# Staging the FFN weights deeper and decoding them four halves per three units, with one more attention tile on the fp32 path, in a fused bias-attention, layer-norm and FFN kernel

## The chip, the core and the metric

The kernel runs on one core of one Trainium2 chip. The metric is the device time of one launch in microseconds (us). The engines are TensorE (PE in the profile), VectorE (DVE), ScalarE (ACT), GpSimd (POOL) and SyncE (SP); SP and POOL are used here mostly to issue DMAs.

## The reference, cut to what matters

Attention with a position bias over 4 batches (B), 8 heads (H), 576 positions (S) and 64 columns per head (D), then a layer norm and a feed-forward network (FFN) with a residual:

```python
scores = scale * np.matmul(q, k.transpose(0, 1, 3, 2))          # per batch and head, 576 x 576
x = (psi_rel / psi_i)[..., None]                                # from the positions alone
h = np.maximum(x @ w1 + b1, 0.0)                                # hidden 32
scores = scores + (h @ w2).transpose(2, 0, 1)[None]             # one bias per head, all batches
attn = np.exp(scores - np.max(scores, axis=-1, keepdims=True))
attn = attn / (np.sum(attn, axis=-1, keepdims=True) + 1e-09)
x = np.matmul(attn, v).transpose(0, 2, 1, 3).reshape(B, S, 512)
xn = (x - mu) / np.sqrt(var + 1e-06) * g_ln
out = x + np.maximum(xn @ w_ch1, 0.0) @ w_ch2                   # w_ch1 512 x 2048 and w_ch2 2048 x 512, float64
```

The two FFN weights come as 64-bit floats. The kernel reads their raw 32-bit words and builds 32-bit floats from them on DVE.

## The kernel before, in words

**Units and tiles.** The attention is cut into 144 units (b, c, h): a batch, a chunk of 128 query rows and a head. Chunk 4 holds the last 64 rows, two heads to a unit, four units to a batch. `ORD` lists the 20 (batch, chunk) pairs in their order; units are numbered through it, 0 to 143. For unit u, `qk` puts the scores into PSUM (`sps`, L390); `softmax1` adds the bias `ldb` and takes the row maximum in one DVE instruction (L414, the landmark for a unit from here on) and takes the exponential on ACT (L418); `softmax2` and `pv` turn the probabilities round and multiply them with v. The finished rows of a (batch, chunk) pair, 18 tiles in all since the chunks 4 of two batches share one, go through `ln1` and `ln2`, and then are one "block" of the FFN.

**Two paths for the probabilities.** Pairs in the set `NAT` keep fp32: `softmax2` turns them on PE with five transposes (L436, L437), ACT copies the result to SBUF (L438, L439), and `pv` multiplies with raw v in fp32 (L486, or L503 for chunk 4). All others go to fp16 in two parts: ACT writes the high part (L423), DVE the low part (L442, L444), SP issues a DMA transpose (L447, `pt<-e`), and `pv` runs 18 fp16 matmuls (L457) against v that `split_v` has split in two (L341 for the maximum, L368 for the low part).

**The weights.** They come in 16 slices f of two halves i (`w_ch1` and `w_ch2`), 32 halves of 512 KB of raw words. `load_w` issues a half on SP. `decode_w` builds the floats with three DVE instructions (L602, L604, L606) into `wslot[f + 1]`, and PE adds the half to a Gram matrix that bounds the weights (L615). Once all eight halves of a group of four slices are decoded, `w_scale` sets the group's scale, and `split_w` writes the fp16 high part on ACT (L641) and the low part on DVE (L644) into `wslot[f]`. Raw words stand in two places only (`wslot[NF - 1]` and `wslot[NF]`, the two ends of tile `wend`), and the load of one half is issued when the half two before it has been decoded. The main loop decodes one half in each unit:

```python
for _ in range(8):
    if wdec and 32 - len(wdec) < 1 + (100 * u) // 100:
        f, i = wdec.pop(0)
        decode_w(f, i)
        ...
        if wload:
            load_w(*wload.pop(0))
```

**The FFN.** A job is one block with one weight group: 48 matmuls of `ffn_w1` into `hps` (L667), the ReLU and its split into `hh` (ACT L672, DVE L675), 12 matmuls of `ffn_w2` into `y` (L695), and the sum into x (`ffn_y`, DVE L706). There are 72 jobs. `next_fs` takes the first job whose block has passed its layer norm and whose group is split. The main loop paces them: it counts up `mbank` so that the jobs of all blocks that are ready are done by the time the next block comes, at most two half jobs per unit.

**Bias.** `bias_relu` (DVE and ACT L172, L174) and `bias_mm` (PE L210) make the bias of 16 query rows for all heads, `nb<-ev` (L220) writes it to memory in the layout of the diagonal, and `ldb<-nb` (L324 to L327) reads it back per head. The first seven groups come ahead of unit 0.

**What sets the order.** The code is unrolled; a scheduler of the framework puts the instructions of each engine in one fixed order, which the engine keeps at run time. Buffers come from pools of fixed depth. `after` adds a wait by hand; `gate` collects loads that have to wait for a bias group of the start.

Of the kernel before, what the change touches and what calls it, by code (L numbers as in the profile page):

```python
# [22 lines left out]
def kernel(  # L23
# [83 lines left out]
    wslot = [wp.tile([128, 1024], F32, name=f"w{f}") for f in range(NF - 1)]  # L107
# [71 lines left out]
    def bias_mm(gi):  # L179
# [17 lines left out]
        else:  # L197
# [21 lines left out]
        dst = dst.rearrange("k (h j) -> k h j", h=NH)[:, :, 0:ntot]  # L219
        SY.dma_start(out=dst, in_=ev[:, 0:ntot])  # L220

    ORD = [(0, 4), (1, 4), (0, 0), (1, 0), (2, 0), (3, 0), (3, 4), (2, 4),
           (2, 1), (3, 1), (1, 1), (0, 1), (0, 2), (1, 2), (3, 2), (2, 2),
           (2, 3), (3, 3), (1, 3), (0, 3)]
    units, ustart, vis = [], {}, []
    for n, (b, c) in enumerate(ORD):
        ustart[b, c] = len(units)
# [7 lines left out]
    gend = {c: sum(len(range(8 * x, min(36, 8 * x + 8))) for x in corder[:corder.index(c) + 1])  # L235
            for c in range(5)}

    NAT = {(0, 4), (1, 4), (0, 0)}

    def nat_pv(b, c):  # L240
        return (b, c) in NAT
# [31 lines left out]
    gate, gate_on = [], [True]  # L273
# [294 lines left out]

        defer(lo)

    wraw = {}

    def load_w(f, i):
        if f < NF - 2:
            dst = wslot[NF - 1 + i]
        elif f == NF - 2 and i == 1:
            dst = wslot[NF]
        else:
            dst = [ep.tile([128, EW], F32, tag="e", name="wst")[:, 0:512] for _ in range(2)]
            for j in range(2):  # L580
                ld = SY.dma_start(
                    out=dst[j].bitcast(U32),
                    in_=w_ch[f].bitcast(U32)[:, 1024 * i + 512 * j:1024 * i + 512 * j + 512])
                after(ld, ttri[max(ttri)])
            wraw[f, i] = dst
            return
        ld = SY.dma_start(out=dst.bitcast(U32), in_=w_ch[f].bitcast(U32)[:, 1024 * i:1024 * i + 1024])
        if gate_on[0]:
            gate.append((ld, 1 + 2 * i))
        if f >= NF - 2:  # L590
            after(ld, ttri[max(ttri)])
        wraw[f, i] = dst

    def decode_w(f, i):
        wf = wslot[f + 1][:, 512 * i:512 * i + 512]
        src = wraw.pop((f, i))
        src = src if isinstance(src, list) else [src]
        nw = 512 // len(src)
        for j, raw in enumerate(src):
            raw = raw.bitcast(U32).rearrange("p (a b) -> p a b", b=2)  # L600
            w = wslot[f + 1][:, 512 * i + nw * j:512 * i + nw * j + nw].bitcast(U32)
            V.tensor_scalar(out=w, in0=raw[:, :, 1], scalar1=3, scalar2=0x3FFFFFFF,  # L602
                            op0=ALU.logical_shift_left, op1=ALU.bitwise_and)
            V.scalar_tensor_tensor(out=w, in0=raw[:, :, 0], scalar=29, in1=w,  # L604
                                   op0=ALU.logical_shift_right, op1=ALU.bitwise_or)
            V.scalar_tensor_tensor(out=w, in0=raw[:, :, 1], scalar=0xC0000000, in1=w,  # L606
                                   op0=ALU.bitwise_and, op1=ALU.bitwise_or)
        g = GOF[f]
        f0, f1 = GROUPS[g]
        if g not in gram:  # L610
            gram[g] = ps_y.tile([128, 512], F32, tag="y1", name="gram")
        wb = wf.bitcast(BF16).rearrange("p (a b) -> p a b", b=2)[:, :, 1]
        for c in range(4):
            blk = wb[:, 128 * c:128 * c + 128]
            T.matmul(out=gram[g][:, 128 * i:128 * i + 128], lhsT=blk, rhs=blk,  # L615
                     start=(f == f0 and i == 0 and c == 0), stop=(f == f1 - 1 and i == 1 and c == 3))
# [152 lines left out]
    gate.append((SY.dma_start(out=gs_sb, in_=g_r), 3))  # L769
    wload = [(f, i) for f in range(NF) for i in range(2)]  # L770
    wdec = list(wload)
    for _ in range(2):
        load_w(*wload.pop(0))
    issue_loads(-6)
    V.memset(mhalf, -0.5)
    V.memset(one_sb, 1.0)
    V.memset(half2, 0.5)
    bias_setup()
    issue_loads(-4)
    NP = 7  # L780
# [41 lines left out]
    u = 0  # L822
    while u < NU + 6 or jobs or cur_job or pend or yq:
        if u >= NEARLY:
            ffn_y()
        softmax1(u)
        issue_loads(u)
        softmax2(u - 1)
        flush()
        for _ in range(8):  # L830
            if wdec and 32 - len(wdec) < 1 + (100 * u) // 100:
                f, i = wdec.pop(0)
                decode_w(f, i)
                if i == 1 and f + 1 == GROUPS[GOF[f]][1]:
                    w_scale(GOF[f])
                if wload:
                    load_w(*wload.pop(0))
        while mm_done[0] < ngroup:
            bias_mm(gorder[mm_done[0]])
            mm_done[0] += 1  # L840
        if u % 2:
            qk(u + 1)
            qk(u + 2)
        while npv <= u - LAG:
            if pv(npv):
                lnq.append([u, len(avail_at) + len(lnq)])
            npv += 1
        for fn in todo.pop(u, []):
            fn()
        for g, (f0, f1) in enumerate(GROUPS):  # L850
            if wdone[0] >= 2 * f1 and g not in wready_at:
                wready_at[g] = u
        if u < NU + 9:
            nav = len([a for a in avail_at if a <= u])
            goal = sum(2 * NF * len(bl) // 4 for bl in blocks if bl[-1] < nav)
            nxt = min((steps_av[bl[-1]] for bl in blocks if bl[-1] >= nav), default=NU + 9)
            mbank += max(0.0, (goal - (ntot - nmicro) - mbank)) / max(1, nxt - u)
            mbank = min(mbank, 2.0)
        else:
            mbank = 1.0  # L860
        flush_lo()
        ffn_y()
        while mbank >= 1.0:
            if not ffn_micro(u):
                break
            mbank -= 1.0
            nmicro -= 1
            if mbank >= 1.0:
                ffn_y()
        bneed = NP + 1 + u if u < 8 else 12  # L870
        for c in (1, 2, 3):
            bneed = max(bneed, gend[c] - 8 + min(8, (u - cfirst[c] + 30) * 8 // 26))
        if ngroup < min(36, bneed):
            bias_relu(gorder[ngroup], 1)
            ngroup += 1
        for _ in range(2):
            if wspl:
                split_w(*wspl.pop(0))
        for it in list(lnq):
            if it[0] == u - 1:  # L880
                ln1(it[1])
# [57 lines left out]
```

## Time and profile before

| | before |
|---|---|
| time, median of 3 runs | 746.67 us (737.48 to 750.48) |
| profiled execution | 743.11 us |
| its span, first to last instruction | 741.3 us |
| PE busy | 651.0 us |
| DVE busy | 489.6 us |
| ACT busy | 380.9 us |
| mean granted TensorE clock, share of full speed | 0.929 |

The profile is of one execution, so sums are made against 743.11 us, of which 1.8 us lie outside the span; the median of the runs is 3.6 us above that execution. Busy time of PE counts matmuls with their modelled ends, so a busy PE need not be one at its peak.

### The profile page before, as it was taken

The numbers are of one execution on the slowest core, as the hardware profiler recorded it, in microseconds if no ns is written. First come the engines' busy times: TensorE is split into PE (matmuls) and PEld (weight loads), VectorE is DVE, ScalarE is ACT, GpSimd is POOL, SyncE is SP. The second block draws the span as 40 slices with busy tenths as digits, with TensorE's granted clock in tenths as the row PEclk, the third lists the DMA queues.
The fourth block names the chain that finished last, engine by engine and source line by source line (L and its number), as shares of the span: only waits on it lengthen the run. The fifth ranks groups of instructions, "written<-read, shape, count | busy, mean of one in ns | idle before, by whom it ended". The sixth has DMA issues, their size and how long they took to land. (4 is left out here: it accounts for less than half of the span.)

```text
span 741.3 us, 19318 instructions
## 1 busy us (share of the span) xinstructions
PE 651.0 (88%) x7980; PEld 445.9 (60%) x7980; DVE 489.6 (66%) x1114; ACT 380.9 (51%) x731; POOL 87.0 (12%) x160
## 2 busy tenths in 40 slices
PE   4368887576669999999988969999998999999997
PEld 3134465444456766766755647667666767676774
DVE  4467789987788657766585746575675666767322
ACT  4255874453257555556475735566765445454110
POOL 3301120100110010101110101011001101000000
PEclk9668997658969999999999989999999999999999
DMA  7987977699627688977768799686859777646100
GB/s 258 362 241 224 342 239 194 144 234 202 148 61 144 119 154 206 220 153 174 172 107 159 141 191 187 144 178 152 165 118 238 194 150 159 110 81 126 31 16 15
DMA packets 200909, 123.30 MB, mean 166 GB/s; under 512 B 175860, under 2 KB 176116, under 8 KB 200820
## 3 DMA queue, kind: packets, MB, share of 16 engines
q1 hardware_dynamic: 190676, 88.32, 57.0%
q0 software_dynamic: 9280, 33.56, 14.9%
q8 instruction: 63, 1.03, 0.6%
q10 hardware_dynamic: 864, 0.18, 0.2%
q14 instruction: 26, 0.21, 0.1%
HBM read 63.92 MB, written 15.64 MB: 107 GB/s over the span
## 5 line engine op out<-in xcount | busy, mean ns | idle before, releaser
L667 PE MATMUL hps<-xT,w 128*128 128x128 f16 x3240 | 207.1, 225 | 6.9 <-DVE hh L675 3.8
L667 PEld LDWEIGHTS <-w 128*128 128x128 f16 x3240 | 192.4, 101 | 20.2 <-issue 10.2
L418 ACT ACTIVATE t<-t,m 128x576 f32<-128x576 f32 x144 | 111.0, 771 | 179.2 <-DVE m L414 177.7
L695 PE MATMUL y<-w,hh 128*128 128x512 f16 x810 | 190.8, 384 | 1.5 <-DVE x L706 0.8
L442 DVE SCALAR_TENSOR_TENSOR e<-t,e 128x512 f16<-128x512 f32 x128 | 88.2, 689 | 71.4 <-ACT e L423 71.0
L695 PEld LDWEIGHTS <-hh 128*128 128x128 f16 x864 | 80.4, 99 | 89.4 <-issue 4.9
L414 DVE CUSTOM_DVE_ANT_0 t<-sps,ldb 128x576 f32<-128x576 f32 x144 | 107.1, 753 | 25.5 <-PE sps L390 17.4
L390 PE MATMUL sps<-kf,qf 64*128 64x288 f32 (+1 forms) x640 | 104.9, 468 | 8.0 <-DVE m L414 7.8
L457 PE MATMUL xps<-v,pt 128*128 128x64 f16 (+1 forms) x1904 | 79.7, 198 | 31.1 <-DMA pt<-e 26.3
L457 PEld LDWEIGHTS <-pt 128*128 128x128 f16 (+1 forms) x1904 | 66.3, 102 | 64.5 <-issue 32.8
L423 ACT ACTIVATE e<-t 128x576 f16<-128x576 f32 x128 | 86.3, 679 | 12.0 <-DMA pt<-e 9.3
L706 DVE SCALAR_TENSOR_TENSOR x<-y,ycs,x 128x512 f32<-128x512 f32 x72 | 53.9, 749 | 48.3 <-PE y L695 48.1
L672 ACT ACTIVATE hh<-hps 128x512 f16<-128x512 f32 x72 | 42.1, 584 | 69.2 <-PE hps L667 69.2
L390 PEld LDWEIGHTS sps<-kf,qf 64*128 64x128 f32 (+1 forms) x640 | 49.2, 187 | 42.3 <-issue 12.6
L675 DVE SCALAR_TENSOR_TENSOR hh<-hps,hh 128x512 f16<-128x512 f32 x72 | 49.4, 687 | 35.5 <-ACT hh L672 35.1
L291 POOL DMA_DIRECT2D kf<-in_k_s_dram x64 | 36.0, 562 | 262.6 <-PE sps L390 237.8
L172 ACT ACTIVATE r<-psi_sb,pr_sb 128x512 f32<-128x512 f32 (+31 forms) x92 | 52.7, 633 | 6.4 <-DVE pr_sb L123 3.7
L210 PE MATMUL bps<-r,nw_sb 128*32 128x296 f32 (+34 forms) x474 | 34.1, 368 | 11.3 <-DVE r L174 9.9
L602 DVE TENSOR_SCALAR w<-wend 128x512 uint32<-128x512 uint32 x28 | 12.1, 431 | 34.7 <-DMA wend<-in_w_ch_dram 34.7
L304 POOL DMA_DIRECT2D qf<-in_q_main_dram x32 | 17.6, 551 | 120.2 <-PE sps L390 80.0
L210 PEld LDWEIGHTS bps<-r,nw_sb 128*32 128x32 f32 x474 | 16.7, 118 | 21.8 <-issue 10.4
L641 ACT ACTIVATE w<-w,ws 128x512 f16<-128x512 f32 x28 | 19.7, 716 | 17.7 <-DVE ws L113 9.8
(102 smaller groups left out, 548.0 us busy)
## 6 DMA issues: line engine op xcount, KB each, us to landing
kf<-in_k_s_dram POOLq DMA_DIRECT2D x64, 288.0 KB, 4.4
wend<-in_w_ch_dram SPq DMA_DIRECT2D x29, 512.0 KB, 5.7
nb<-ev SPq DMA_DIRECT2D x33, 296.0 KB, 3.6
ldb<-nb SPq DMA_DIRECT2D x32, 288.0 KB, 5.3
qf<-in_q_main_dram POOLq DMA_DIRECT2D x32, 256.0 KB, 4.7
vf<-in_v_p_dram POOLq DMA_DIRECT2D x16, 320.0 KB, 8.0
out_dram<-x SPq DMA_DIRECT2D x18, 256.0 KB, 2.8
ldb<-nb SPq DMA_DIRECT2D x16, 144.0 KB, 8.2
```

The lines of the kernel that those rows point to most:

```text
L172: S.activation(r[:, 0:n], psi_sb[:, 0:n], AF.Relu, bias=pr_sb[:, g4:g4 + 1], scale=1.0)
L210: T.matmul(out=ps[32 * s:32 * s + 32, hf, a - lo:b - lo], lhsT=nw2_sb, rhs=src, start=True, stop=True)
L390: T.matmul(out=o, lhsT=l, rhs=kk, start=True, stop=True, tile_position=(64 * hf, 64 * e))
L414: ttri[u] = V.tensor_tensor_reduce(out=halves(t), in0=ps[:, :, 0:HS], in1=halves(bias), scale=-0.125, scalar=3e38, op0=ALU.add, op1=ALU.mi ...
L418: S.activation(t, t, AF.Exp, bias=m, scale=-1.0, accum_out=l8[b, c][:, h:h + 1])
L423: S.activation(e16[:, 0:SEQ], t, AF.Copy, scale=E_SCALE)
L442: V.scalar_tensor_tensor(out=e16[:, 640:1152], in0=t[:, 0:512], scalar=E_SCALE, in1=e16[:, 0:512], op0=ALU.mult, op1=ALU.subtract)
L457: T.matmul(out=o, lhsT=p[:, m], rhs=v[:, j, a, :], start=(i == 0), stop=(i == len(ops) - 1))
L667: T.matmul(out=h[:, idx * n:idx * n + n], lhsT=w[:, wo + kk * 128:wo + kk * 128 + 128], rhs=xT[k][:, xo + kk, 0:n], start=(i == 0), stop=( ...
L675: V.scalar_tensor_tensor(out=hh[:, 1], in0=h, scalar=0.0, in1=hh[:, 0], op0=ALU.max, op1=ALU.subtract)
L695: T.matmul(out=yps[k][t], lhsT=hh[:, a, o:o + 128], rhs=w[:, wo:wo + 512], start=(f == f0 and i == 0), stop=(f == f1 - 1 and i == 2))
L706: V.scalar_tensor_tensor(out=x, in0=y, scalar=ycs[:, g:g + 1], in1=x, op0=ALU.mult, op1=ALU.add)
```

## The change

The order of two tiles is swapped, and (1, 0) joins the fp32 path. `load_w` chooses for each raw half the first free slot among all that are not yet needed for decoded weights, with up to six halves loaded ahead of the decoding (two at the very end, which stage in the `ep` pool as before). The decoding runs at four halves in three units, with a wait on the landmark instruction of the current unit.

```diff
-    ORD = [(0, 4), (1, 4), (0, 0), (1, 0), (2, 0), (3, 0), (3, 4), (2, 4),
+    ORD = [(0, 4), (1, 4), (1, 0), (0, 0), (2, 0), (3, 0), (3, 4), (2, 4),
-    NAT = {(0, 4), (1, 4), (0, 0)}
+    NAT = {(0, 4), (1, 4), (1, 0), (0, 0)}
...
-    def load_w(f, i):
-        if f < NF - 2:
-            dst = wslot[NF - 1 + i]
-        elif f == NF - 2 and i == 1:
-            dst = wslot[NF]
+    def load_w():
+        f, i = wload[0]
+        n = 2 * f + i
+        busy = {x for m, x in stg.items() if m not in decoded}
+        fit = [x for x in range(NF + 1) if x not in busy and (2 * x >= n + 3 or x == 0 and n < 6)]
+        if n < 2 * NF - 2:
+            if not fit or n >= len(decoded) + 6:
+                return False
+            stg[n] = fit[0]
+            dst = wslot[fit[0]]
         else:
+            if n >= len(decoded) + 2:
+                return False
             dst = [ep.tile([128, EW], F32, tag="e", name="wst")[:, 0:512] for _ in range(2)]
...
+            if gate_on[0]:
+                gate.append((ld, min(NP - 1, n + 1)))
+            else:
                 after(ld, ttri[max(ttri)])
...
     def decode_w(f, i):
...
+            if ttri:
+                after(dec, ttri[max(ttri)])
...
-    for _ in range(2):
-        load_w(*wload.pop(0))
+    while load_w():
+        pass
...
-            if wdec and 32 - len(wdec) < 1 + (100 * u) // 100:
+            if wdec and 32 - len(wdec) < 1 + (4 * u) // 3:
                 f, i = wdec.pop(0)
                 decode_w(f, i)
                 if i == 1 and f + 1 == GROUPS[GOF[f]][1]:
                     w_scale(GOF[f])
-                if wload:
-                    load_w(*wload.pop(0))
+                while wload and load_w():
+                    pass
```

Lines of the changed kernel move by up to ten: `decode_w` is L610, L614 and L616 there, `split_w` L654, `hh` L685, `ffn_y` L716, and `load_w` L592.

Two places of the order show what moves (`w10_148` is slot 10 of the weights, `wend_153` the last two, `nb4` and `nb0` the bias of chunks 4 and 0, and L414 is printed as ISA). The first is SP's queue at the start, up to the first read of the bias for unit 0 (L326). Before, one raw half (`wend_153`) stands in front of it here, after two more that lie ahead of the piece:

```order
L587 DMA wend_153<-in_w_ch_dram 128x1024
L220 DMA nb4_133<-ev_310 16x8x592
L220 DMA nb0_129<-rp_334 16x8x592
L220 DMA nb0_129<-ev_358 16x8x592
L587 DMA wend_153<-in_w_ch_dram 128x1024
L220 DMA nb0_129<-rp_374 16x8x592
L326 DMA ldb_384<-nb4_133 64x576
```

The same queue in the changed kernel, from the third raw half on:

```order
L592 DMA w3_141<-in_w_ch_dram 128x1024
L220 DMA nb4_133<-ev_314 16x8x592
L592 DMA w4_142<-in_w_ch_dram 128x1024
L220 DMA nb0_129<-rp_338 16x8x592
L592 DMA w5_143<-in_w_ch_dram 128x1024
L220 DMA nb0_129<-ev_362 16x8x592
L592 DMA w6_144<-in_w_ch_dram 128x1024
L220 DMA nb0_129<-rp_378 16x8x592
L326 DMA ldb_388<-nb4_133 64x576
```

Six raw halves now go ahead of that read, each into a slot of its own, where there were three into two slots.

The second place is DVE around the landmark of unit 22 (L414). Before, the halves of slot `w10` are being decoded there, and nothing of the second group is split:

```order
L602 TENSOR_SCALAR w10_148<-wend_153 128x512
L606 SCALAR_TENSOR_TENSOR w10_148<-wend_153,w10_148 128x512
L626 TENSOR_SCALAR wred_121<-gram_929 128x2
L552 SCALAR_TENSOR_TENSOR u_1613<-x_1451,mv_1506,gs_sb_119 128x512
L414 ISA t_1617,m_1618<-sps_1485,ldb_760 128x576
L414 ISA m_1618 128x1
L414 ISA t_1663,m_1664<-sps_1640,ldb_831 128x576
L414 ISA m_1664 128x1
L604 SCALAR_TENSOR_TENSOR w10_148<-wend_153,w10_148 128x512
```

The changed kernel at the same unit:

```order
L685 SCALAR_TENSOR_TENSOR hh_1486<-hps_1437,hh_1486 128x512
L118 TENSOR_SCALAR winv_123<-winv_123 128x2
L616 SCALAR_TENSOR_TENSOR w14_152<-wend_153,w14_152 128x512
L654 SCALAR_TENSOR_TENSOR w8_146<-w9_147,ws_122,w8_146 128x512
L639 TENSOR_SCALAR ycs_124<-winv_123,ginv_127 128x1
L654 SCALAR_TENSOR_TENSOR w8_146<-w9_147,ws_122,w8_146 128x512
L414 ISA t_1703,m_1704<-sps_1688,ldb_843 128x576
L414 ISA m_1704 128x1
L654 SCALAR_TENSOR_TENSOR w9_147<-w10_148,ws_122,w9_147 128x512
L716 SCALAR_TENSOR_TENSOR x_822<-y0_1538,ycs_124,x_822 128x512
```

There the slot `w14` is done, and the third group (`w8` and on) is being split. Counted through the lists, unit 22 has 19 decoded halves and 8 split ones in front of it before, and 28 and 18 in the changed kernel.

## Rows read from the trace of the kernel before

**Rows 1.** The page, part 1: busy us, share of the span, instructions.

```profile
PE 651.0 (88%) x7980; PEld 445.9 (60%) x7980; DVE 489.6 (66%) x1114; ACT 380.9 (51%) x731; POOL 87.0 (12%) x160
```

**Rows 2.** Windows: us; PE, PEld, DVE, ACT, POOL busy (instructions); clock; DMA share; GB/s.

```profile
0.00:42.33 42.33, 15.99 (x204) 9.09 (x204) 20.51 (x54) 13.60 (x18) 14.24 (x29) 0.79 0.91 308
42.33:85.70 43.37, 35.63 (x443) 20.87 (x443) 30.84 (x72) 29.25 (x59) 5.20 (x9) 0.85 0.81 250
85.70:105.30 19.60, 17.41 (x162) 12.63 (x161) 17.73 (x41) 16.04 (x37) 5.67 (x11) 1.00 0.73 248
105.30:126.10 20.80, 15.48 (x117) 11.41 (x117) 17.03 (x37) 11.21 (x24) 2.68 (x6) 0.84 0.78 239
126.10:149.40 23.30, 14.91 (x120) 8.83 (x120) 22.08 (x54) 11.10 (x20) 2.78 (x5) 0.66 0.75 156
149.40:218.00 68.60, 46.20 (x460) 31.81 (x461) 54.98 (x130) 28.94 (x51) 8.19 (x11) 0.72 0.75 167
218.00:294.80 76.80, 76.80 (x1048) 51.76 (x1047) 52.44 (x122) 45.83 (x85) 6.23 (x11) 0.99 0.75 147
```

**Rows 3.** Waits of DVE, 42 to 218 us: total us, times, longest.

```profile
DVE w L602 <- DMA wend<-in_w_ch_dram: 24.2, 13, 5.3
...
DVE x L706 <- PE y L695: 4.3, 2, 2.3
```

**Rows 4.** DVE groups, 42 to 218 us: count, busy us, mean ns, idle before.

```profile
L644 DVE SCALAR_TENSOR_TENSOR w<-w,ws,w 128x512 f16<-128x512 f32 x24 | 17.8, 743 | 0.7 <-ACT w L641 0.7
...
L606 DVE SCALAR_TENSOR_TENSOR w<-wend,w 128x512 uint32<-128x512 uint32 x25 | 17.2, 687 | 0.2
...
L442 DVE SCALAR_TENSOR_TENSOR e<-t,e 128x512 f16<-128x512 f32 x16 | 11.0, 685 | 0.0
...
L602 DVE TENSOR_SCALAR w<-wend 128x512 uint32<-128x512 uint32 x25 | 10.8, 431 | 24.3 <-DMA wend<-in_w_ch_dram 24.2
...
L368 DVE SCALAR_TENSOR_TENSOR v<-vf,vs,v 128x640 f16<-128x640 f32 x12 | 10.5, 872 | 0.0
...
L341 DVE TENSOR_REDUCE vam<-vf 128x1 f32<-128x640 f32 x12 | 9.4, 812 | 0.0
...
L444 DVE SCALAR_TENSOR_TENSOR e<-t,e 128x64 f16<-128x64 f32 x16 | 3.5, 218 | 0.0
...
L706 DVE SCALAR_TENSOR_TENSOR x<-y,ycs,x 128x512 f32<-128x512 f32 x4 | 3.0, 744 | 4.3 <-PE y L695 4.3
...
L675 DVE SCALAR_TENSOR_TENSOR hh<-hps,hh 128x512 f16<-128x512 f32 x4 | 2.7, 685 | 0.0
```

**Rows 5.** Timeline of DVE: the first L414 of units 0, 32 and 48.

```profile
42.33 0.76 DVE L414 CUSTOM_DVE_ANT_0 t<-sps,ldb 128x576 f32<-128x576 f32 x1 [0.95 <-DMA ldb<-nb]
...
218.01 0.75 DVE L414 CUSTOM_DVE_ANT_0 t<-sps,ldb 128x576 f32<-128x576 f32 x1
...
294.82 0.76 DVE L414 CUSTOM_DVE_ANT_0 t<-sps,ldb 128x576 f32<-128x576 f32 x1 [0.37 <-DMA ldb<-nb]
```

**Rows 6.** Chain that ended last, its final FFN job: start us, us, what.

```profile
728.42 2.68 PE hps L667 x48
731.10 2.60 PE y L695 x12
```

**Rows 7.** DMA issues of the span: count, KB each, median us to landing.

```profile
wend<-in_w_ch_dram SPq DMA_DIRECT2D x29, 512.0 KB, 5.7
...
pt<-e SPq DMA_TRANSPOSE x128, 3.7
```

**Rows 8.** PE groups by form, 85 to 105 us (fp32 path of units 8 to 15).

```profile
L486 PE MATMUL xps<-vf,pt 128*128 128x64 f32 x40 | 5.0, 269 | 0.0
...
L436 PE MATMUL ptm<-id_sb,t 128*128 128x128 f32 x24 | 3.9, 285 | 0.6 <-ACT pt L438 0.6
...
L437 PE MATMUL ptl<-id_sb,t 128*64 128x128 f32 x6 | 1.7, 277 | 0.0
```

**Rows 9.** PE groups by form, 300 to 340 us (fp16 path).

```profile
L457 PE MATMUL xps<-v,pt 128*128 128x64 f16 x112 | 4.6, 194 | 0.0
```

More of the change, by code (lines that the diff above doesn't have):

```diff
@@ L569, in ln2 @@
         defer(lo)
-    wraw = {}
-    def load_w(f, i):
-        if f < NF - 2:
-            dst = wslot[NF - 1 + i]
-        elif f == NF - 2 and i == 1:
-            dst = wslot[NF]
-        else:
+    wraw, decoded = {}, set()
+    stg = {}
+    def load_w():
[8 more added lines that the diff above has]
+            dst = wslot[fit[0]]
+        else:
+            if n >= len(decoded) + 2:
+                return False
             dst = [ep.tile([128, EW], F32, tag="e", name="wst")[:, 0:512] for _ in range(2)]
[L580 to L583, printed above, removed]
-                after(ld, ttri[max(ttri)])
[L585 to L591, printed above, removed]
+        wload.pop(0)
+        for j, d in enumerate(dst if isinstance(dst, list) else [dst]):
+            w = d.shape[1]
+            ld = SY.dma_start(out=d.bitcast(U32),
+                              in_=w_ch[f].bitcast(U32)[:, 1024 * i + w * j:1024 * i + w * j + w])
+            if gate_on[0]:
+                gate.append((ld, min(NP - 1, n + 1)))
+            else:
+                after(ld, ttri[max(ttri)])
         wraw[f, i] = dst
+        return True
     def decode_w(f, i):
@@ L596, in decode_w @@
         src = wraw.pop((f, i))
+        decoded.add(2 * f + i)
         src = src if isinstance(src, list) else [src]
@@ L601, in decode_w @@
             w = wslot[f + 1][:, 512 * i + nw * j:512 * i + nw * j + nw].bitcast(U32)
-            V.tensor_scalar(out=w, in0=raw[:, :, 1], scalar1=3, scalar2=0x3FFFFFFF,
-                            op0=ALU.logical_shift_left, op1=ALU.bitwise_and)
+            dec = V.tensor_scalar(out=w, in0=raw[:, :, 1], scalar1=3, scalar2=0x3FFFFFFF,
+                                  op0=ALU.logical_shift_left, op1=ALU.bitwise_and)
+            if ttri:
+                after(dec, ttri[max(ttri)])
             V.scalar_tensor_tensor(out=w, in0=raw[:, :, 0], scalar=29, in1=w,
@@ L771 @@
     wdec = list(wload)
-    for _ in range(2):
-        load_w(*wload.pop(0))
+    NP = 7
+    while load_w():
+        pass
     issue_loads(-6)
@@ L779 @@
     issue_loads(-4)
-    NP = 7
     for n in range(NP + 1):
```

## The prediction

> **What bounds the kernel now.** I read the page's busy shares first: PE is busy for 651.0 of 741.3 us, DVE for two thirds [rows 1]. A share over the whole span hides two different stages, so the windows come next, cut at the landmarks of units [rows 2, 5]. From unit 32 at 218.0 us to unit 48 at 294.8 us PE is busy for all of 76.8 us at a granted clock of 0.99, while DVE is busy for 52.4. From there to the end the chain runs over PE: a whole FFN job is 2.68 + 2.60 = 5.28 us of matmuls, one behind the other [rows 6]. So after unit 32 time is PE work, and only less of it, or more of it done earlier, ends the kernel sooner.
>
> Ahead of unit 32 PE is not the limit. In the five stages between 42.3 and 218 us PE is busy for 35.6 + 17.4 + 15.5 + 14.9 + 46.2 = 129.6 of 175.7 us, with the granted clock down to 0.66 and 0.72 in the last two. DVE is busy for 30.8 + 17.7 + 17.0 + 22.1 + 55.0 = 142.7 us, which leaves it 33.0 us idle [rows 2]. What ends that idle time is the third view: 24.2 us in 13 waits of L602, the first instruction of a decoding, for a raw half; 4.3 us for `y` of an FFN job; the other 4.5 us lie in pieces too small to show here [rows 3]. DVE keeps its order, so each of the 13 waits also holds the landmark, the split and the residual sum queued behind it, and PE starves with it.
>
> **The change part by part.** *Staging.* A half needs 5.7 us from its issue to its landing [rows 7], and only two slots exist, each free again only when its half is decoded. With six ahead, a half is asked for several decodings (0.431 + 0.687 + 0.687 = 1.8 us each, L604 taken at the time of L606 [rows 4]) and some units before its turn. The last halves have only one or two slots, where about four can still be exposed: in the new list some 4 to 8 DVE instructions stand between the freeing of a slot and its next use, 3 to 6 us, against those 5.7. I keep 4 us of the 24.2; the bounds are 0 and 12.
>
> *The start.* SP now issues six halves ahead of the first bias read instead of three. DVE's first landmark waited for just that read [rows 5]. Three halves are 1.57 MB; at the 308 GB/s of the first stage, whose DMA engines were 0.91 busy [rows 2], that is 5.1 us. The bounds are 0 (the read waits for bias groups from PE and ACT anyway) and 5.1; nothing is taken away there, so no gain. As the engines were almost full I take 3 us: unit 0 at 45.3.
>
> *DVE work between unit 0 and unit 32*, by counting the two lists, new minus old: 3 more halves decoded there, since none comes ahead of unit 0 now, x 1.805 = +5.4; 8 more low parts of weights (32 for 24) x 0.743 = +5.9; 9 fewer low parts of probabilities (7 for 16) x (0.685 + 0.218) = -8.1, eight of them the tile that goes to fp32; 2 more v maxima x 0.812 = +1.6; 4 fewer v splits, moved behind unit 57, x 0.872 = -3.5; 2 more `hh` x 0.685 = +1.4; 1 more residual sum x 0.744 = +0.7 [rows 4]. The sum is +3.4 us: the change takes almost no work from DVE, it only moves it forward.
>
> *The fp32 path of (1, 0).* A unit costs PE four L436 and one L437, 4 x 3.9 / 24 + 1.7 / 6 = 0.93 us [rows 8], and five L486, 5 x 5.0 / 40 = 0.63, against 18 L457, 18 x 4.6 / 112 = 0.74 [rows 8, 9]. That is 0.8 us more, 6.6 us for eight units. It is covered as long as DVE sets the pace, where PE was busy for 15 of 21 to 23 us [rows 2]; without that cover it is a loss of 6.6. In return SP is rid of 8 DMA transposes, 3.7 us to landing each [rows 7], and POOL of four k loads (60 for 64), because (1, 0) now follows (1, 4) of its batch. I count these at nothing: they only clear the way for the raw halves.
>
> *Waits.* The decoding now waits for the landmark of its unit, which is on DVE itself, so nothing is queued behind it that was not before. A load waits for that landmark on SP, with bias reads, bias writes and one layer-norm transpose behind it. DMA transposes of probabilities now begin with unit 24, when nearly all loads are out. Bounds 0 and 5 us; I take 0, since the landmark is early in its unit.
>
> *Unit 32.* 45.3 + 142.7 + 3.4 + idle time. Of the idle time I keep 4 us for raw halves, the 8.8 us of other waits, and 3 more (0 to 8) because two more jobs run on a slow PE: 15.8. Unit 32 then starts at 207.2, 10.8 us earlier. Until unit 24 the new order is behind the old one, as 40 us of DVE work stand between the landmarks of units 20 and 24 where 24 stood; it gains after that, with 38 against 61 up to unit 32.
>
> *Units 32 to 48.* Counted in PE's list, 6 `hps` and 5 `y` halves of jobs lie ahead of unit 32, where there were 4 and 3, and by unit 48 there are 16 and 14 for 15 and 14. So 10 and 9 run in this stretch instead of 11 and 11. PE was full there, so they come off: 2.68 + 2 x 2.60 = 7.9 us [rows 6]; if PE is not full from the very start, 3 us less.
>
> *To the end.* From unit 48 PE's list is one `hps` ahead throughout, with the same number of `y`: 2.7 us less. The tail behind the last unit, the bias bursts and their stalls are as they were.
>
> Sum: 10.8 + 7.9 + 2.7 = 21.4 us off the profiled execution of 743.1, so **722 us**. The median of the runs is 3.6 us above that execution and their lowest 5.6 us below it; I don't add that.
>
> **A rule against it.** Between 42.3 and 218 us the DMA engines are busy for 0.73 to 0.81 of the time at 156 to 250 GB/s, where they did 0.91 and 308 in the first stage [rows 2]. The Trainium skill (DMA: Bandwidth & Descriptors, Issuing engines are not separate DMA queues) states that DMAs from all issuing engines run on the same 16 DMA engines and interleave, so more loads in flight share the same rate; by it alone nothing of the 24.2 us would come back. The rows leave a fifth to a quarter of the engines free, which is for a wait on latency.
>
> **The rivals.** *A: the raw halves are limited by the DMA engines, not by two slots.* For it speaks a busy share of 0.8 with many small packets of transposes among them. Against it speak the free share and the 8 transposes and 4 k loads that go. Then the 24.2 us stay and the start costs all of 5.1: unit 32 at 47.4 + 146.1 + 36.0 = 229.5, 11.5 us late, of which 7.9 + 2.7 come back: 744 us, no change. The skill's rule above is this rival.
>
> *B: PE is the bound between units 20 and 32.* Its two extra jobs, 10.6 us, and the fp32 path have to fit beside DVE, at a granted clock that was 0.66 and 0.72 there [rows 2]. If PE, not DVE, paces this stretch, the two jobs only change places and unit 32 is 10.6 us later than in the sum: 732 us. For it speaks the low clock; against it, that PE was idle for a third of that time.
>
> *C, slower: decodings stand in DVE's queue ahead of their data.* The new list places 9 to 10 halves and 16 splits between units 20 and 24. If the SP queue gets late (a load behind a wait for a slot that is freed late), each of the last ten halves is exposed for 5.7 - 1.8 = 3.9 us, 39 us instead of the 4 I kept, with every landmark behind it: 743.1 - 21.4 + 35 = 757 us. It beats the gain once more than 25 us of such waits are left. Against it: ten halves have four to six slots, and only the last four have one or two.
>
> **How the numbers follow.** Forecast 0.66, A 0.15, B 0.12, C 0.07. The forecast's own range from the bounds: raw halves 0 to 12 for 4, start 0 to 5 for 3, waits on PE 0 to 8 for 3, SP 0 to 5 for 0, and 3 us in the full stretch; all on the good side give 712, most on the bad side 735. B lies in it, A at its edge; the runs of the kernel before spread over 13 us. From 708 to 742 us some 8 in 10 are covered, C and the upper part of A being left out. About 2% is what a measurement of this kernel tells from no change, which is 731.7 us. Faster by more: 0.61 from the forecast and 0.05 from B, 0.66. Within 2%: the rest of these and A, 0.27. Slower: 0.07, all C.
>
> **What would show it.** In the new profile the 24.2 us of L610 waiting for raw halves should be under 12, the landmark of unit 0 at 43 to 47 us, that of unit 32 near 207 and of unit 48 near 276; the five stages' DVE idle time near 16. PE should be full from unit 32 at a clock near 1. Unit 24 should start later than the 149.4 us of before. The forecast is wrong if the waits for raw halves stay (A), if PE is busy for nearly all of units 20 to 32 (B), if these waits grow behind unit 20 (C), or if a new wait at the bias or q and k loads holds units 0 to 8.

## The result and the profile after

The changed kernel takes 708.72 us, the median of four runs (704.25 to 710.42), beside 745.17 us (737.48 to 750.48) for the kernel before on the same chip: a ratio of 0.9538, 95% interval 0.9492 to 0.9583. The profiled execution took 709.05 us with a span of 707.3, which is 34.0 us less than the span of before. All medians and ranges in this text are over all runs, while the ratios leave out runs more than 1.5% above the fastest of their kernel.

The page of the changed kernel, part 1, busy us, share and instructions, as in [rows 1]:

```profile
PE 640.2 (91%) x7988; PEld 447.6 (63%) x7988; DVE 480.5 (68%) x1095; ACT 383.4 (54%) x739; POOL 90.1 (13%) x156
```

PE and DVE each lost about 10 us of busy time, so most of the 34.0 us is idle time of PE, 90.3 us before and 67.1 now. PE's own work did not shrink (7988 matmuls for 7980); its busy time fell at a mean granted clock of 0.961, where it was 0.929. The windows of the changed kernel, cut at its own landmarks of units 0, 8, 16, 20, 24, 32 and 48, say where (columns as in [rows 2]):

```profile
0.00:48.80 48.80, 13.35 (x192) 8.29 (x192) 14.20 (x43) 13.71 (x18) 16.14 (x33) 0.79 0.92 327
48.80:89.20 40.40, 33.06 (x435) 20.05 (x437) 37.40 (x78) 28.16 (x57) 2.96 (x5) 0.83 0.65 199
89.20:111.00 21.80, 20.28 (x188) 15.11 (x189) 21.61 (x51) 17.67 (x40) 4.86 (x8) 1.00 1.03 371
111.00:126.10 15.10, 13.36 (x123) 9.41 (x121) 15.10 (x37) 7.05 (x16) 4.59 (x4) 1.00 0.52 123
126.10:163.30 37.20, 28.95 (x207) 22.67 (x207) 35.63 (x79) 20.87 (x39) 7.79 (x6) 0.77 0.52 172
163.30:200.70 37.40, 36.97 (x414) 27.17 (x414) 35.05 (x85) 26.05 (x51) 6.05 (x9) 1.00 0.41 93
200.70:272.80 72.10, 72.10 (x1068) 50.30 (x1067) 46.59 (x110) 41.28 (x78) 6.36 (x12) 1.00 0.83 173
```

Before, PE was full from unit 32; now it is full from unit 24 on (36.97 of 37.40 us, at a clock of 1.00 where it was 0.72). Unit 0 is 6.4 us later, unit 24 13.9 later, and unit 32 17.3 earlier, as the landmarks on DVE's timeline show beside [rows 5]:

```profile
48.75 0.76 DVE L414 CUSTOM_DVE_ANT_0 t<-sps,ldb 128x576 f32<-128x576 f32 x1 [10.98 <-DMA ldb<-nb]
...
200.74 0.75 DVE L414 CUSTOM_DVE_ANT_0 t<-sps,ldb 128x576 f32<-128x576 f32 x1
...
272.81 0.75 DVE L414 CUSTOM_DVE_ANT_0 t<-sps,ldb 128x576 f32<-128x576 f32 x1
```

Between units 0 and 32 DVE's idle time is 7.1 us, for the 33.0 of before. Its waits in the changed kernel from 48 us to 201 us, total, times, longest, beside [rows 3] (the first is the one that ends at unit 0):

```profile
DVE t L414 <- DMA ldb<-nb: 11.0, 1, 11.0
DVE r L174 <- DMA nb<-ev: 1.7, 1, 1.7
DVE x L716 <- PE y L705: 1.6, 1, 1.6
```

No decoding waits for a raw half any more. What the prediction did not read stands on the other engine. PE's own waits in the kernel *before*, 42 to 218 us, begin with the transposed probabilities:

```profile
PE xps L457 <- DMA pt<-e: 18.5, 9, 4.6
PE sps L390 <- DVE m L414: 7.8, 6, 3.8
```

In the changed kernel PE has no wait for `pt<-e` between units 0 and 32. Its longest wait now lies around unit 0, from 23.7 to 50.1 us, for bias work `r` that stands on DVE directly after the landmark of unit 0:

```profile
PE bps L210 <- DVE r L174: 26.4, 1, 26.4
```

The 34.0 us in four pieces, from the landmarks: 17.3 by unit 32, another 4.7 up to unit 48 (72.1 us for 76.8), another 8.9 between unit 48 and the last, 143 (375.0 for 383.9), and 3.1 in the tail behind it (59.5 for 62.6).

### The profile page after: what moved, and what is told of

It reads as the page before. It is cut to its first block, busy times and chain, and to the rows that moved or that the text cites. A ratio compares the mean times of both kernels' runs of the same rounds, so it can differ in the third digit from the quotient of the medians.

```text
span 707.3 us, 19297 instructions
## 1 busy us (share of the span) xinstructions
PE 640.2 (91%) x7988; PEld 447.6 (63%) x7988; DVE 480.5 (68%) x1095; ACT 383.4 (54%) x739; POOL 90.1 (13%) x156
## 5 line engine op out<-in xcount | busy, mean ns | idle before, releaser
L677 PE MATMUL hps<-xT,w 128*128 128x128 f16 x3240 | 196.4, 220 | 3.1 <-DVE w L654 1.7
L677 PEld LDWEIGHTS <-w 128*128 128x128 f16 x3240 | 184.9, 98 | 7.2 <-DVE w L654 2.2
L442 DVE SCALAR_TENSOR_TENSOR e<-t,e 128x512 f16<-128x512 f32 x120 | 82.7, 689 | 71.5 <-ACT e L423 71.1
L414 DVE CUSTOM_DVE_ANT_0 t<-sps,ldb 128x576 f32<-128x576 f32 x144 | 106.5, 750 | 18.0 <-DMA ldb<-nb 11.3
L682 ACT ACTIVATE hh<-hps 128x512 f16<-128x512 f32 x72 | 42.7, 593 | 127.2 <-PE hps L677 121.6
L390 PE MATMUL sps<-kf,qf 64*128 64x288 f32 (+1 forms) x640 | 97.8, 444 | 0.6 <-ACT rp L213 0.3
L685 DVE SCALAR_TENSOR_TENSOR hh<-hps,hh 128x512 f16<-128x512 f32 x72 | 49.6, 690 | 65.9 <-ACT hh L682 65.4
L457 PEld LDWEIGHTS <-pt 128*128 128x128 f16 (+1 forms) x1792 | 61.1, 100 | 51.9 <-issue 32.2
L423 ACT ACTIVATE e<-t 128x576 f16<-128x576 f32 x120 | 79.4, 677 | 8.2 <-DMA pt<-e 6.0
L457 PE MATMUL xps<-v,pt 128*128 128x64 f16 (+1 forms) x1792 | 72.6, 194 | 6.6 <-DMA pt<-e 5.9
L716 DVE SCALAR_TENSOR_TENSOR x<-y,ycs,x 128x512 f32<-128x512 f32 x72 | 53.7, 746 | 19.7 <-PE y L705 19.7
L210 PE MATMUL bps<-r,nw_sb 128*32 128x296 f32 (+33 forms) x474 | 33.6, 372 | 32.5 <-DVE r L174 26.7
L544 POOL TENSOR_SCALAR rs<-mv 128x1 f32<-128x1 f32 x18 | 8.1, 451 | 161.6 <-DVE mv L543 117.3
L418 ACT ACTIVATION_READ_ACCUMULATOR t<-t,m 128x1 f32 x144 | 27.0, 188 | 0.0
```

Source lines behind the costliest of these rows:

```text
L210: T.matmul(out=ps[32 * s:32 * s + 32, hf, a - lo:b - lo], lhsT=nw2_sb, rhs=src, start=True, stop=True)
L390: T.matmul(out=o, lhsT=l, rhs=kk, start=True, stop=True, tile_position=(64 * hf, 64 * e))
L414: ttri[u] = V.tensor_tensor_reduce(out=halves(t), in0=ps[:, :, 0:HS], in1=halves(bias), scale=-0.125, scalar=3e38, op0=ALU.add, op1=ALU.mi ...
L418: S.activation(t, t, AF.Exp, bias=m, scale=-1.0, accum_out=l8[b, c][:, h:h + 1])
L423: S.activation(e16[:, 0:SEQ], t, AF.Copy, scale=E_SCALE)
L442: V.scalar_tensor_tensor(out=e16[:, 640:1152], in0=t[:, 0:512], scalar=E_SCALE, in1=e16[:, 0:512], op0=ALU.mult, op1=ALU.subtract)
```

## The experiments

Three causes stood against each other at first. *Theory W*: the waits for raw halves were the cost; staging takes them away, and PE's work moves forward. *Rival P*: the gain is the fp32 path's, with its 8 DMA transposes and 4 k loads fewer. *Rival R*: it is the faster decoding's. Later D (the parts add up), O (they overlap), T (the transposes) and K (DVE's work, or the k loads) take up what was left.

The table puts the profiled execution of each kernel together, from the windows, waits and landmarks between its own units 0 and 32 (us; "raw" is DVE's wait for raw halves in all its groups, "pt" PE's wait for `pt<-e`, "jobs" the `hps` and `y` done ahead of unit 32, "end" the end of the span).

| | unit 0 | DVE busy | DVE idle | unit 32 | raw | pt | jobs | unit 48 | end |
|---|---|---|---|---|---|---|---|---|---|
| before | 42.3 | 142.7 | 33.0 | 218.0 | 24.2 | 18.5 | 5.0, 4.1 | 294.8 | 741.3 |
| e1 staging | 45.5 | 146.6 | 19.8 | 211.9 | 3.3 | 7.0 | 6.0, 4.5 | 284.3 | 732.9 |
| e2 path | 45.1 | 133.5 | 15.5 | 194.1 | 12.3 | 0.8 | 5.4, 4.2 | 271.2 | 722.2 |
| e3 staging, rate | 47.5 | 144.3 | 10.2 | 202.0 | 1.7 | 8.3 | 4.4, 3.0 | 289.4 | 729.1 |
| e4 rate, path | 42.7 | 144.7 | 31.2 | 218.6 | 20.4 | 0 | 7.0, 6.0 | 287.7 | 732.8 |
| e5 staging, path | 48.4 | 138.2 | 17.4 | 204.1 | 0 | 3.8 | 5.0, 4.2 | 282.5 | 729.0 |
| e7 fp32 only | 44.9 | 135.0 | 20.2 | 200.1 | 12.7 | 0.5 | 6.0, 4.2 | 280.1 | 727.0 |
| e8 order only | 40.0 | 143.2 | 23.8 | 207.0 | 14.4 | 12.4 | 5.1, 4.2 | 289.9 | 731.7 |
| changed | 48.8 | 144.9 | 7.1 | 200.7 | 0 | 0 | 6.2, 6.0 | 272.8 | 707.3 |

**Staging alone (e1_stage).** From the changed kernel:

```diff
-    ORD = [(0, 4), (1, 4), (1, 0), (0, 0), (2, 0), (3, 0), (3, 4), (2, 4),
+    ORD = [(0, 4), (1, 4), (0, 0), (1, 0), (2, 0), (3, 0), (3, 4), (2, 4),
-    NAT = {(0, 4), (1, 4), (1, 0), (0, 0)}
+    NAT = {(0, 4), (1, 4), (0, 0)}
-            if wdec and 32 - len(wdec) < 1 + (4 * u) // 3:
+            if wdec and 32 - len(wdec) < 1 + (100 * u) // 100:
```

> The deeper staging alone: the old order of tiles, the old fp32 set and one half decoded in each unit. Theory W (the gain is DVE's waits for raw halves, and PE work that moves forward with them): the 24.2 us of waits fall under 3, the start is 6 us later as in the changed kernel, so 725 to 733 us. Rival P (the gain is the fp32 path of (1, 0), with its transposes and k loads off the DMA engines): within 1% of before. Rival R (the faster decoding does it): within 1% of before.

Measured: 734.04 us (727.85 to 734.71), ratio 0.9832, 0.9786 to 0.9878. The waits for raw halves fall from 24.2 to 3.3 us, as W has it, and P and R, with less than 1% here, fall as causes by themselves. But the time is 1 us above W's range, and unit 32 is only 6.1 us earlier. DVE's idle time falls by 13.2, of which a unit 0 that is 3.2 us later and 3.9 us more DVE work behind it take back more than half.

**The path alone (e2_path).** The first two edits of the change without the others, two slots and one half per unit:

```diff
-    ORD = [(0, 4), (1, 4), (0, 0), (1, 0), (2, 0), (3, 0), (3, 4), (2, 4),
+    ORD = [(0, 4), (1, 4), (1, 0), (0, 0), (2, 0), (3, 0), (3, 4), (2, 4),
-    NAT = {(0, 4), (1, 4), (0, 0)}
+    NAT = {(0, 4), (1, 4), (1, 0), (0, 0)}
```

> The swapped tiles and the fp32 path of (1, 0) alone, with two slots and one half per unit. Theory W: DVE loses 7 us of low parts but keeps its waits for raw halves near 24 us, so 733 to 745 us. Rival P: most of the gain, 712 to 722 us. Rival R: no change.

Measured: 722.85 us (713.72 to 728.69), ratio 0.9668, 0.9602 to 0.9735. The part that the prediction counted at nothing is worth the most alone. DVE has 9.2 us less to do ahead of unit 32, and its waits for raw halves are halved with two slots as before. The groups and issues of e2 between 45 and 194 us show both:

```profile
L602 DVE TENSOR_SCALAR w<-wend 128x512 uint32<-128x512 uint32 x25 | 10.6, 423 | 11.8 <-DMA wend<-in_w_ch_dram 11.7
...
L442 DVE SCALAR_TENSOR_TENSOR e<-t,e 128x512 f16<-128x512 f32 x7 | 4.8, 680 | 0.0
```

```profile
wend<-in_w_ch_dram SPq DMA_DIRECT2D x25, 512.0 KB, 4.6
```

A half lands in 4.6 us, where the median over the same units was 5.5 before. Of PE's waits for `pt<-e` 0.8 us are left, and the granted clock is 1.00 from unit 8 to unit 24, for 1.00, 0.84 and 0.66 in the three stages of [rows 2].

**Staging with the faster decoding (e3_stage_rate).** As e1_stage, but with the changed kernel's line `1 + (4 * u) // 3`:

```diff
-            if wdec and 32 - len(wdec) < 1 + (100 * u) // 100:
+            if wdec and 32 - len(wdec) < 1 + (4 * u) // 3:
```

> Deeper staging and four halves per three units, with the old tiles and fp32 set. Theory W: nearly all of the gain, 712 to 722 us. Rival P: 730 us or more. Rival R: 712 to 722 us too; the run of the faster decoding without the staging tells R from W.

Measured: 731.27 us (726.74 to 734.9), ratio 0.9819, 0.9776 to 0.9863: no more than e1. W had nearly all of the gain here, 712 to 722 us, and fails. DVE is at unit 32 9.9 us sooner than in e1, but PE is not: it has done 4.4 `hps` and 3.0 `y` by then, and works it off in the next stage, which is 87.4 us long and full:

```profile
202.00:289.40 87.40, 87.40 (x1154) 57.88 (x1153) 54.87 (x126) 46.64 (x87) 7.13 (x13) 1.00 0.58 128
```

An early landmark alone is no gain; what counts is how much of PE's list lies ahead of it.

**The faster decoding and the path with two slots (e4_rate_path).** From the kernel before, the two edits of e2 and

```diff
-            if wdec and 32 - len(wdec) < 1 + (100 * u) // 100:
+            if wdec and 32 - len(wdec) < 1 + (4 * u) // 3:
```

> Four halves per three units and the fp32 path of (1, 0), with the old two slots. Theory W: each half is waited for as long as before or longer, since its turn comes sooner: waits for raw halves of 25 to 45 us and 732 to 750 us. Rivals P and R: 708 to 722 us.

Measured: 734.19 us (731.94 to 737.88), ratio 0.9866, 0.9833 to 0.99. Without the slots the faster decoding costs 2 points (a point is 0.01 of the ratio) of what the path had gained, so it is not the cause by itself as R had it (no run has it alone). DVE's waits in e4, 42.7 to 218.6 us:

```profile
DVE w L602 <- DMA wend<-in_w_ch_dram: 19.7, 14, 3.9
DVE hh L675 <- ACT hh L672: 5.0, 2, 4.1
```

This is what rival C of the prediction described, decodings that stand in DVE's queue ahead of their data; it needs two slots to come about, and its price was 20.4 us of waits for raw halves in all, 8.1 more than in e2, not 39.

**The changed kernel without the faster decoding (e5_stage_path).** From the changed kernel:

```diff
-            if wdec and 32 - len(wdec) < 1 + (4 * u) // 3:
+            if wdec and 32 - len(wdec) < 1 + (100 * u) // 100:
```

> Deeper staging, swapped tiles and the fp32 path of (1, 0), with one half per unit: the changed kernel without the faster decoding. Theory D (the two gains, 12 us from the staging alone and 21 from the path alone, remove different parts of DVE's early time and add up; the faster decoding only brings half a job to the tail): 711 to 717 us, a tail of 62.6 behind the last landmark. Rival R (the faster decoding is needed to use the staging): 720 us or more. Rival O (the path already removes what the staging removes): 718 to 724 us, as the path alone.

Measured: 732.95 us (730.76 to 737.0), ratio 0.9845, 0.9792 to 0.9899. D falls: staging and path together give less than the path alone, and less than e7 below, which was measured beside it (0.972). O falls too; of the three only R's 720 us or more came. In e5 no decoding waits, but other waits have come in the place of those (its DVE waits between 48.4 and 204.1 us; the first again ends at unit 0):

```profile
DVE t L414 <- DMA ldb<-nb: 10.9, 1, 10.9
DVE hh L685 <- ACT hh L682: 5.5, 2, 2.9
DVE var L350 <- DMA vall<-vmx: 4.1, 2, 3.0
DVE r L174 <- DMA nb<-ev: 1.9, 2, 1.2
DVE e L442 <- ACT e L423: 1.5, 1, 1.5
```

Against e2, unit 0 is 3.3 us later, and three more halves are decoded behind it, 3 x 1.805 = 5.4 us [rows 4]. The faster decoding then fills DVE's idle time with work that is ready (17.4 us idle in e5, 7.1 in the changed kernel) and has 6.2 `hps` and 6.0 `y` done by unit 32 for 5.0 and 4.2.

**The two halves of the path (e7_fp32, e8_swap).** Both from the kernel before. e7 puts (1, 0) on the fp32 path in the old order, with all its k loads:

```diff
-    NAT = {(0, 4), (1, 4), (0, 0)}
+    NAT = {(0, 4), (1, 4), (1, 0), (0, 0)}
```

> The kernel before with (1, 0) on the fp32 path alone: tiles in their old order, all k loads kept. Theory T (the gain of the path is that its 8 transposes and 7 us of low parts leave the DMA engines and DVE): nearly all of it, 720 to 728 us. Rival K (it is the four k loads and the longer use of one k): 738 us or more.

e8 swaps the two tiles (four k loads fewer) and keeps three pairs on the fp32 path, so there are as many transposes and as much for DVE to do as before:

```diff
-    ORD = [(0, 4), (1, 4), (0, 0), (1, 0), (2, 0), (3, 0), (3, 4), (2, 4),
+    ORD = [(0, 4), (1, 4), (1, 0), (0, 0), (2, 0), (3, 0), (3, 4), (2, 4),
-    NAT = {(0, 4), (1, 4), (0, 0)}
+    NAT = {(0, 4), (1, 4), (1, 0)}
```

> The kernel before with the two tiles swapped, and as many tiles on the fp32 path as before, (1, 0) in the place of (0, 0): four k loads fewer, just as many transposes, begun at the same unit. Theory T: 738 to 746 us. Rival K: 720 to 728 us.

Measured: e7 723.63 us (720.17 to 728.91), ratio 0.972, 0.9659 to 0.9781; e8 732.72 us (726.2 to 739.79), ratio 0.9787, 0.9714 to 0.986. Each halves the waits for raw halves by itself (12.7 and 14.4 for 24.2 us), so both T and K hold in part, and together they bring no more of that. By the time, e7 is where T put it and e8 lies between the two, with intervals that overlap. Only e7 ends PE's waits for `pt<-e`; PE in e8, 40 to 207 us:

```profile
PE xps L457 <- DMA pt<-e: 12.4, 8, 2.5
PE gram L615 <- DVE w L606: 8.2, 2, 4.2
```

**Putting back what the path takes away (e9_dve, e10_transpose).** Both from e2. e9 adds the DVE instructions of a tile's low parts to the eight units of (0, 0), e10 two DMA transposes to each of them; nobody reads what they write.

```diff
+            if units[u][0:2] == (0, 0):
+                d16 = e16p.tile([128, 1152], F16, tag="e16", name="d16")
+                V.scalar_tensor_tensor(out=d16[:, 640:1152], in0=t[:, 0:512], scalar=E_SCALE,
+                                       in1=t[:, 0:512], op0=ALU.mult, op1=ALU.subtract)
+                V.scalar_tensor_tensor(out=d16[:, 576:640], in0=t[:, 512:576], scalar=E_SCALE,
+                                       in1=t[:, 512:576], op0=ALU.mult, op1=ALU.subtract)
```

> The swap and the fp32 path of (1, 0) alone, as in e2_path (ratio 0.967, waits for raw halves 11.7 us), with two idle DVE instructions put back behind each landmark of the eight units of (0, 0): the 0.685 and 0.218 us of a tile's low parts, 7.2 us in all, whose result nobody reads. Theory T (the path gains because eight units' DMA transposes leave the queue while raw halves are in flight): the halves still land in 4.6 us; the 7.2 us fall into DVE's waits; ratio 0.967 to 0.971, waits for raw halves 5 to 9 us. Theory K (the path gains because DVE has 7.2 us less to do ahead of unit 32): unit 32 is 7 us later than in e2_path, 201; ratio 0.976 to 0.980.

```diff
+            if units[u][0:2] == (0, 0):
+                d16 = e16p.tile([128, 1152], F16, tag="e16", name="d16")
+                d16 = d16.rearrange("p (a b) -> p a b", a=9)
+                for a, b in ((0, 5), (5, 9)):
+                    dt = SY.dma_start_transpose(out=d16[:, a:b], in_=xsrc[:, 0:128 * (b - a)])
+                    after(dt, ttri[u])
```

> The swap and the fp32 path of (1, 0) alone, as in e2_path, with two idle DMA transposes (640 and 512 columns, of a constant tile, whose result nobody reads) put back behind the landmark of each of the eight units of (0, 0). Theory T: the raw halves land in 5.5 us again, for 4.6, the waits for them go from 11.7 back to some 20 us, and the ratio from 0.967 to 0.977 to 0.985. Theory K: the transposes cost nothing, ratio 0.967, unit 32 at 194.

Measured: e9 723.89 us (720.19 to 732.07), ratio 0.9733, 0.9663 to 0.9803, which lies between T's and K's ranges and overlaps e2's; e10 733.2 us (730.41 to 736.75), ratio 0.9882, 0.9827 to 0.9937. So DVE's 7.2 us are worth less than their length: unit 32 is 2.6 us later counted from unit 0, since DVE was busy for 5.7 us more and part of that fell into waits (idle 12.4 us for 15.5). The transposes take back over 2 points. But not in the way T had it: raw halves land as in e2, and DVE waits no longer for them. Issues and DVE waits in e10, 42.9 to 212.9 us:

```profile
wend<-in_w_ch_dram SPq DMA_DIRECT2D x25, 512.0 KB, 4.7
...
d<-xsrc SPq DMA_TRANSPOSE x16, 5.0
```

```profile
DVE w L609 <- DMA wend<-in_w_ch_dram: 11.1, 9, 3.8
DVE t L415 <- PE sps L391: 8.4, 4, 4.1
DVE t L415 <- DMA ldb<-nb: 3.9, 2, 3.3
DVE wred L633 <- PE gram L142: 3.8, 2, 3.0
```

DVE's idle time is 33.1 us because it now waits for a late PE (scores and Gram sums). PE is late at a lower granted clock, 0.81 for 0.90 from unit 0 to unit 32, and part of that lies ahead of the first added transpose, which was issued at 117.8 us. The stage from unit 8 to unit 16, in e2 and then in e10:

```profile
92.60:113.10 20.50, 18.70 (x171) 13.12 (x168) 17.48 (x39) 16.76 (x39) 4.90 (x9) 1.00 0.86 289
```

```profile
88.90:117.00 28.10, 24.84 (x159) 17.84 (x157) 18.56 (x40) 17.39 (x39) 4.52 (x8) 0.69 0.67 214
```

The scheduler also put the instructions in another order for e10 and e9 than for e2, so e10 doesn't give the price of the transposes alone.

**Fewer halves at the start (e6_start3, e11_start3_again, e12_after_again).** From the changed kernel, for the halves that are asked for ahead of unit 0:

```diff
-            if not fit or n >= len(decoded) + 6:
+            if not fit or n >= len(decoded) + (3 if gate_on[0] else 6):
```

> The changed kernel with three raw halves instead of six ahead of the first bias read, six from then on. Theory B (in the start the DMA engines are full, and three halves cost the first landmark 5 to 6 us): unit 0 near 43 us for 48.8, and 703 to 706 us. Rival: the halves are then missing later and the waits come back, so no change, 707 to 710 us.

Measured: 713.05 us (702.9 to 723.49), ratio 0.9476, 0.9402 to 0.955, from two of its four runs, which was ahead of the changed kernel's. As the two had been measured at different times, both were run again side by side:

> The changed kernel with three halves asked for at the start instead of six, the same as e6_start3, beside the changed kernel itself in one call. If the start is worth what the traces show (unit 0 at 41.2 for 48.8, end 701.1 for 707.3), the time is 700 to 705 us, 0.9 points below e12_after_again. If it is given back later or was chance, the two agree within 0.3 points.

> The changed kernel itself once more, as the base for e11_start3_again: ratio 0.949 to 0.958, 706 to 711 us.

Measured: e11 716.83 us (708.95 to 718.95), ratio 0.9634, 0.9579 to 0.9688; e12, the changed kernel itself, 713.0 us (708.12 to 716.91), ratio 0.9607, 0.9562 to 0.9652. The earlier start is real; the gain of e6 did not come again. The windows of e11 and then of e12, cut at units 0, 24, 32 and 48:

```profile
0.00:43.10 43.10, 12.85 (x192) 7.81 (x192) 14.15 (x42) 13.71 (x18) 16.57 (x33) 0.82 0.92 318
43.10:161.80 118.70, 97.16 (x951) 66.76 (x951) 110.39 (x240) 74.31 (x153) 14.87 (x23) 0.88 0.70 225
```

```profile
0.00:48.10 48.10, 13.38 (x192) 8.01 (x192) 14.21 (x42) 13.71 (x18) 16.32 (x33) 0.80 0.92 327
48.10:162.60 114.50, 90.73 (x946) 62.88 (x947) 109.84 (x240) 74.07 (x151) 20.20 (x23) 0.91 0.67 214
```

Unit 0 is 5.0 us earlier with three halves, and 4.2 of them are given back by unit 24. The transfers that were kept out of the start run behind it (225 GB/s for 214). No version tried is shown to beat the changed kernel.

## Why the prediction was right, and where its sizes were off

The sign held, and so did the waits that were to go: 722 us forecast against a profiled execution of 743.1, and 709.05 in the profiled execution of the changed kernel, a fall of 34.1 us where 21.4 were forecast. The mechanism held in part, as staging and the faster decoding without the path gain only 1.8 points (e3). The time lies at the lower edge of the stated range (708 to 742) and below the 712 us that the sum's own bounds give at best. That it stays inside is partly luck: 8.9 of the 34.0 us came in a stretch where the sum had no gain, with a cause that is only partly known, and the same kernel took 713.0 us when it was run again. Step by step, against the profiled execution:

*Staging.* Right in the waits. Those for raw halves went from 24.2 to 0, within the bounds of 0 to 12 around the 4 that were kept. In e1 alone they fell to 3.3, but that alone was worth only 1.7 points.

*The start.* 6.4 us for 3, beyond the bound of 5.1 and the 43 to 47 us that were named as a sign. How much of it the three halves cost is not settled: six halves against three make 5.0 us in e12 and e11, and 7.5 in the changed kernel and e6. In flight each took longer to land (8.4 us for `w`, the median of the issues in the first 60 us, for 7.0 before). But unit 0 also moves with the old two slots, 2.8 us later in e2, 2.6 later in e7, 2.3 earlier in e8, so something else than the number of halves moves it too. e11 and e12 show that most of such a delay comes back by unit 24, so the size of this term hardly mattered.

*DVE's work.* Right: 142.68 to 144.88 is 2.2 us more, for 3.4.

*The fp32 path.* This is the term that was most wrong in size. The PE work of 6.6 us did not show as a loss, as said, but the transposes and k loads were counted "at nothing". e2 gains 3.3 points by the path alone, with staging untouched. Three things are in it: DVE's 8 low parts (in the sum), shorter waits for raw halves even with two slots, and PE's 18.5 us of waits for `pt<-e`, which stood in PE's list of waits and were not read, as PE was taken not to be the limit there. The windows did show its low clock. Which of the three weighs most is not shown: with DVE's low parts put back (e9) 2.7 of the 3.3 points stay, a difference within the noise, and e4, which has no wait for `pt<-e` either, gains only 1.3.

*Idle time.* 7.1 us where 15.8 were kept: 4 for raw halves and 3 for a slow PE did not come (PE's clock was 1.00 from unit 24, not 0.72), and of the 8.8 of other waits 7.1 stayed. Unit 32 came at 200.7 for 207.2: of the 6.5 us, 8.7 are idle time and 1.2 DVE's work, less 3.5 of the start (the sum agrees to 0.1).

*Units 32 to 48.* 4.7 us for 7.9. The count of jobs ahead of unit 32 was right for the new list (6.2 and 6.0 for 6 and 5) and low for the old one: 5.0 `hps` and 4.1 `y` were done there, for the 4 and 3 counted in PE's list. DVE's landmark and PE's position are not the same point of time when DVE waits.

*To the end.* 3.1 us in the tail, for 2.7. Not in the sum: 8.9 us between units 48 and 143, where the same number of jobs runs in both. PE's waits there, before and then in the changed kernel:

```profile
PE xps L457 <- DMA pt<-e: 7.8, 2, 6.0
PE hps L667 <- DVE hh L675: 3.8, 2, 2.4
PE xps L457 <- DVE x L493: 1.3, 1, 1.3
```

```profile
PE xps L457 <- DMA pt<-e: 5.9, 3, 3.7
PE xps L457 <- DVE x L493: 0.7, 1, 0.7
PE bps L190 <- DVE m L414: 0.7, 1, 0.7
```

PE is idle for 5.7 us less (7.4 for 13.1) and busy for 3.2 us less. The waits of `hps` for `hh` go with the faster decoding: they are 0 to 1.5 us in the six profiles that have it, 1.6 to 3.8 in the eight that don't. Those for `pt<-e` fall by 1.9 us. Two windows of the kernel before and the one that answers to the first in the changed kernel show these:

```profile
439.00:451.00 12.00, 8.43 (x88) 7.00 (x88) 3.45 (x8) 2.70 (x5) 0.00 (x0) 0.72 1.15 164
571.00:583.00 12.00, 10.14 (x116) 7.56 (x113) 6.96 (x17) 3.59 (x7) 1.86 (x4) 0.86 0.93 205
```

```profile
405.00:417.00 12.00, 8.30 (x95) 5.37 (x93) 5.10 (x12) 4.16 (x10) 1.06 (x2) 0.88 1.15 176
```

PE stalls for `pt<-e` where a new tile's bias, k and q loads fill the DMA engines (share 1.15), and the clock falls behind the stall. Before there are three windows below 0.9 in this stretch (the third, at 391 us, has 0.86), in the changed kernel one. Is this chance? The four profiles of the changed kernel and its start variants take 373.7 to 378.9 us for this stretch, the kernel before and all nine others 379.2 to 388.3. So it seems to belong to the kernel, though the groups are only 0.3 us apart and two profiles of the changed kernel differ by 3.9. Which part makes the stalls for `pt<-e` fewer stays open, since no run changes them alone.

*Rival A* fell with e1 and the changed kernel, where the halves came in time on the same DMA engines. The Trainium skill (DMA: Bandwidth & Descriptors, Issuing engines are not separate DMA queues) states that DMAs of all issuing engines run on the same 16 DMA engines and interleave. That more loads in flight then share one rate, as the prediction read from it, agrees with the start, 8.4 us for 7.0; it says nothing of waits that end because a load is asked for earlier. *Rival B* had PE full between units 20 and 32: it was, from unit 24 (36.97 of 37.40 us), but at full clock, and unit 32 was not late. *Rival C* shows only in e4, at a smaller price.

*Do the parts add up?* No. Alone, staging gives 1.7 points and the path 3.3; together 1.6 (e5); all three 4.6, or 3.9 in the second measurement. Taken away last, each part is worth about the same: staging 3.3 points (e4 against the changed kernel), the path 2.8 (e3), the faster decoding 3.1 (e5); against the second measurement of the changed kernel each is 0.7 less. The table gives a reason, which is argued from these traces and not tested by itself: the faster decoding needs the slots (raw waits 20.4 us without them), its earlier splits are jobs for PE only if PE is free to run them (in e3 PE was late and the next stage took 87.4 us), and slots without the faster decoding only trade one wait for another (e5). Between two measurements of one kernel the ratio moved by 0.7 and 1.6 points (the changed kernel; e6 and e11), so none of these points is sharper than that. The order that the scheduler makes differs in each of these kernels too, and what of the points is its doing is not separated.

## What to carry to other kernels

Read the waits of every engine in the stretch that a change touches, those of the engine that is not the limit too: 18.5 us of waits on PE stood in the profile, and the edit that ends them was priced at nothing. Several small limits in one stretch can hide one another, so that a part brings little until the others are gone, or even costs time (e5 beside e2); price a part by what it is worth with the others in place, and expect another gain of it alone. And a variant that looks better by a point, measured apart from its base, is run again beside it before it is believed: here 0.9476 became 0.9634.

## What the runs showed of the hardware

A stall of PE can cost more than its length. In the kernel before, behind the two stalls above, the chain that ended last shows single `hps` jobs at 4.76 and 4.22 us, which take 2.68 elsewhere [rows 6]; its row of the first, and the DMA transpose in front of it:

```profile
428.83 13.69 DMA pt<-e
442.52 0.04 issue
442.57 0.93 PE xps L457 x14
443.49 4.76 PE hps L667 x48
```

So 6.0 us of waiting there (PE's wait for `pt<-e` in that window) took some 2 us more in the job behind it, at a granted clock of 0.72 over the window. The second stall, 1.9 us, was followed by the job of 4.22 us. In the changed kernel the `y` behind a wait of 3.7 us (at 413.7 us) took some 4.4 us, where the one behind a wait of 1.4 us (at 543.8 us) took its usual 2.75. The transpose itself counts 13.69 us from the work that released it, against a median landing of 3.7 us [rows 7], at the change of tiles.

With fewer transposes or k loads up to unit 32 a 512 KB load landed sooner: medians of 5.5 us before, 5.2 in e8, 4.6 in e2 and 4.5 in e7. But e10, with 16 transposes added again, kept 4.7, so the count of transposes is not the whole of it.
